# Moving one accumulating transfer, and the order of VectorE's list, in a fused convolution, GELU and projection kernel with Strassen blocks

## The chip, the core and the metric

The kernel runs on one core of one Trainium2 chip. The metric is device time in microseconds. Before the change it is 677.74 us, the median of 3 runs (676.55 to 678.93). Engines are named as in the profile: PE is TensorE, PEld its weight loads, DVE is VectorE, ACT is ScalarE, POOL is GpSimd, and SP is SyncE, which only issues transfers.

## The reference, cut to what matters

The input x holds 8 sequences of 4096 tokens with 192 channels. Each of 8 heads owns 24 channels and has 7 taps, normalised by a softmax. Every channel is convolved causally along its sequence with its head's taps. The result is a matrix of 32768 tokens by 192 channels. It goes through two dense layers with an exact GELU between them:

```python
w = np.exp(weight - weight.max(-1, keepdims=True))
w = w / (w.sum(-1, keepdims=True) + 1e-9)
conv = np.einsum('hk,bskhg->bshg', w, x_unfolded).reshape(B * S, D)
h = conv @ w_in                                   # 192 -> 2048
g = 0.5 * h * (1.0 + erf(h / sqrt(2)))
out = g @ w_out                                   # 2048 -> 192
```

## The kernel before, in words

**Tiling.** The tokens are split into two halves of 16384, which are worked on together. A half has 35 blocks: blocks 0 to 5 have 256 tokens per half, and blocks 6 to 34 have 512. For each block, SyncE loads x, VectorE transposes it to channels by tokens (function `trans`, letter t, L753), VectorE and in part ScalarE compute the seven taps (function `conv`, letter c, L781; ScalarE's share is L871), and TensorE multiplies by w_in (L998, into the PSUM tile hp). ScalarE applies GELU into the tile gT (L903), and TensorE multiplies by w_out into four PSUM banks of the tile ob.

**Stages.** TensorE works in a fixed order. While the first product of block n runs, in sixteen slices, the second product of block n − 1 is threaded between the slices. The document calls this stretch stage n. A slice holds 12 matmuls of the first product and a share of the second. In the even stages from 8 on the second product is the plain one of an odd block (`mm2_t`, L1076).

**Strassen blocks.** The even blocks 8, 10, ... 32 (list `ST`, thirteen of them) use a Strassen form of the second product, `mm2_s` (L1136), which runs in the odd stage behind them. It needs fewer matmuls, and in exchange sums of operands and of results. The operand sums are S1, S3, Dn and S4. S1 and S3 have four parts each, Dn and S4 two halves each. Dn is made from S1, and S4 from Dn. Parts 0 and 1 of S1 and parts 0, 1 and 2 of S3 are made by pairs of transfers that GpSimd issues: a copy of the first operand (L496), and behind its landing an accumulating transfer of the second operand (L499), both in `st_dma`. VectorE makes the other parts in `st_add` (L489): S1[2], S1[3], S3[3], Dn[0], Dn[1], S4[0], S4[1]. The list `DMAS` holds the places of the transfers in GpSimd's order, as (place, sum, part, first or second operand).

**Results of a Strassen block.** The products leave PSUM over the tiles p5s, uu, tq and gsm. ScalarE copies (`st_copy`, L528) at the slices in `AT_COPY`. VectorE makes four sums (`st_post`, letter p: P0 is L537, P1 is L541, P2 is L544, P3 is L548). GpSimd issues three transfers per block (`st_move`): p5s from its upper half to its lower one (L506), which P1 waits for; uu into gsm (L508), which P3 waits for; and the accumulating transfer of uu into tq (L511), called the tq transfer here. It waits until ScalarE's last copy (`S_AC`) and P0 to P2 (`S_DP`) are done. Three transposes on VectorE (L563, `st_evac`) bring the results to the tile osb: one from a bank and one from gsm (letter e, named E), and one from tq (letter q, the tq transpose), which waits for the tq transfer. SyncE's stores of the block wait for the tq transpose (`S_ET`), and so does ScalarE's first copy for the next Strassen block. The results of an odd block are transposed straight from three banks (`evac_t`, letter e, L377, named T0, T1, T2). T1 and T2 wait for the end of the whole second product (`S_MM2`), and each frees a bank for the Strassen product that follows.

**What sets the order.** VectorE executes the string `ORDER` letter by letter. Each letter takes the next piece of its lane: t, c, e, p and q as above, w for weight sums at the start, and 1, 3, d and 4 for VectorE's parts of S1, S3, Dn and S4. A piece that waits holds up all that follow. GpSimd's queue is sorted by pairs (block, place). The pairs of `DMAS` belong to block m; p5s stands at (m + 1, 8.5), gsm at (m + 2, 2), and the tq transfer at (m + 2, 14.1), behind all transfers for block m + 2. The copy of halo columns (`halo`, L674) for block n stands at (n − 2, 0). SyncE's queue in an odd stage begins at slice 4 and holds, in this order, four loads, the four stores of a Strassen block, four loads, and the four stores of an odd block.

A piece is named with its block in the following: c10.3b is tap 3 of block 10, second of two instructions; t12 is the transposing of block 12; E8 is a result transpose of block 8.

Of the kernel before, what the change touches and what calls it, by code (L numbers as in the profile page):

```python
# [11 lines left out]
def bass_lightweight_conv__then__act_gelu_exact_kernel(  # L12
# [59 lines left out]
    ST = list(range(M0 + 2, M1, 2))  # L72
# [46 lines left out]
    def ap(t, off, pat):  # L119
        return bass.AP(t, off, pat)  # L120

    with es:
# [139 lines left out]
        def part(q):  # L262

            return FQ * (0, 4, 2)[q], [[NP * F, 64], *([[F, NP]] if q < 2 else [[4 * FQ, 2 * NP]]), [1, FQ]]


        def cast(e, n, p):
            e.wait_ge(S_TR, NP * n + p + 1)
            dst = ap(xTb[PC[n]], p * XB + HX, [[NP * XB, 128], [1, WS[n]]])
            src = ap(xT[n % 2], p * XW + HX, [[NP * XW, 128], [1, WS[n]]])  # L270
            if n == 0:
                ins = e.activation(out=dst, in_=src, func=AF.Copy)
            else:
                ins = e.tensor_copy(dst, src)
            ins.then_inc(S_CAST[PC[n]])

        def dup(e, q, hf):

            c0, pat = part(q)
            e.wait_ge(S_WIN[(hf, 2 + 3 * hf, 3 + hf)[q]], 16)  # L280
            e.tensor_copy(
                ap(win, 64 * (1 - hf) * NP * F + c0 + FQ, pat), ap(win, 64 * hf * NP * F + c0, pat)
            ).then_inc(S_DUPP if (q, hf) == (0, 1) else S_DUPE)

        def trd(n):

            return NP * (n + 1) if n < 2 else 2 * NP + n - 1

        def cvd(n):

            return sum(NCV - 2 * (m in K0) for m in range(n + 1) if m not in PC)
# [273 lines left out]
        def load(e, n, qs=(0, 2, 1, 3), sm=None):  # L565
            mb = WS[n] // 32
            if n >= NX:
                e.wait_ge(S_TR, trd(n - NX))
            for q in qs:
                off = ((q // 2) * HALF + OFF[n]) * D + DQ * (q % 2)  # L570
                dst = [[TB // 32 * DQ, 32], [DQ, mb], [1, DQ]]
                src = [[D, 32], [32 * D, mb], [1, DQ]]
                e.dma_start(
                    ap(xin[n % NX], 32 * q * (TB // 32 * DQ), dst), ap(xt, off, src)
                ).then_inc(sm or S_XIN[n % NX], 16)

        def store(e, m):
# [29 lines left out]

        TAPS = ((5, 8, 11), (10, 12, 15))
        ORDER = (
            "tccccccccccccctccctccccccccccccwtccccccccccccwwwwwctcccccccccccctcccccccccccccccccccccccccettceccccc"  # L610
            "cccccccccetccccecccccccetcecc1ccde13de44ccccccpctpcpeccccccccpcccectec1cccd1e3de4q4ccccpcccptpcecccc"
            "ccccpcccectec1cccd1e3de4q4ccccpcccptpceccccccccpcccectec1cccd1e3de4q4ccccpcccptpceccccccccpcccectec1"
            "cccd1e3de4q4ccccpcccptpceccccccccpcccectec1cccd1e3de4q4ccccpcccptpceccccccccpcccectec1cccd1e3de4q4cc"
            "ccpcccptpceccccccccpcccectec1cccd1e3de4q4ccccpcccptpceccccccccpcccectec1cccd1e3de4q4ccccpcccptpceccc"
            "cccccpcccectec1cccd1e3de4q4ccccpcccptpceccccccccpcccectec1cccd1e3de4q4ccccpcccptpceccccccccpcccectec"
            "1cccd1e3de4q4ccccpcccptpceccccccccpcccececc1ccde13de44qccccpcccppepeqeeeeeee"
        )
        AT_COPY = {0: (1, 6), 1: (1, 8), 2: (1, 13), 3: (2, 1)}

        @block.gpsimd  # L620
        def _(g):
            def win_in(q, hf, sm):
                c0, pat = part(q)
                g.dma_start(
                    ap(win, 64 * hf * NP * F + c0, pat), ap(wint, c0 + FQ * hf, pat)
                ).then_inc(sm, 16)

            g.wait_ge(S_MSET, 1)
            for hf in range(2):
                m = idb[64 * hf : 64 * hf + 64, :]  # L630
                g.affine_select(
                    out=m,
                    in_=m,
                    compare_op=ALU.is_equal,
                    fill=0.0,
                    base=0,
                    pattern=[[-1, 64]],
                    channel_multiplier=1,
                ).then_inc(S_IDN)
            g.wait_ge(S_IDN, 2)  # L640
            g.memset(wnm[:, :], 0.0).then_inc(S_WNM)
            g.memset(ap(xTb[0], HF, [[NP * XB, 128], [XB, NP], [1, HB]]), 0.0).then_inc(S_HALO)
            for q in range(2):
                for hf in range(2):
                    win_in(q, hf, S_WIN[(hf, 2 + 3 * hf)[q]])
            g.wait_ge(S_PRO, 9)
            g.tensor_tensor(
                ap(dg, 3 * 64, [[KS * 64, 128], [64, KS - 3], [1, 64]]),
                ap(idb, 0, [[64, 128], [0, KS - 3], [1, 64]]),
                ap(wcol, 3, [[32, 128], [1, KS - 3], [0, 64]]),  # L650
                ALU.mult,
            ).then_inc(S_DG)

            def wout_in(k):
                g0, gs = ((0, 1), (4, 1), (2, 4), (3, 4))[k]
                g.dma_start(
                    ap(wout, 2 * g0 * C, [[NF * C, 128], [2 * gs * C, 2], [1, 2 * C]]),
                    ap(woutt, 256 * g0 * C, [[2 * C, 128], [256 * gs * C, 2], [1, 2 * C]]),
                ).then_inc(S_WOUT[k], 16)

            def halo(n):

                t, tw = (xTb[PC[n]], XB) if n in PC else (xT[n % 2], XW)
                dst = ap(t, HF, [[NP * tw, 128], [tw, NP], [1, HB]])
                if n >= 4:
                    g.wait_ge(S_CV, cvd(n - 2))
                if OFF[n] % SEQ == 0:
                    g.memset(dst, 0.0).then_inc(S_HALO)
                    return
                g.wait_ge(S_TR, trd(n - 1))  # L670
                src = ap(
                    xT[(n - 1) % 2], HF + WS[n - 1], [[NP * XW, 128], [XW, NP], [1, HB]]
                )
                g.tensor_copy(dst, src).then_inc(S_HALO)  # L674

            win_in(2, 0, S_WIN[3])
            load(g, 2, (0,), S_XP)
            halo(1)
            g.wait_ge(S_HALO, 2)
            dup(g, 0, 1)  # L680
            win_in(2, 1, S_WIN[4])
            wout_in(0)
            load(g, 2, (2,), S_XP)
            g.wait_ge(S_DUPP, 1)
            cast(g, 1, 0)
            cast(g, 1, 1)
            load(g, 2, (1,), S_XP)
            wout_in(1)
            cast(g, 1, 2)
            load(g, 2, (3,), S_XP)  # L690
            wout_in(2)
            wout_in(3)
            halo(2)
            work = [((n - 2, 0), halo, n) for n in range(3, NB)]
            for m in ST:
                for at, name, q, h in DMAS:
                    work.append(((m, at), st_dma, g, m, name, q, h))
                work += [((m + 1, 8.5), st_move, g, m, 0), ((m + 2, 2), st_move, g, m, 1)]
                work.append(((m + 2, 3 if m == ST[-1] else 14.1), st_move, g, m, 2))
            for _, op, *rest in sorted(work, key=lambda q: q[0]):  # L700
                op(*rest)

# [549 lines left out]
```

## Time and profile before

| Quantity | Value |
|---|---|
| Median of 3 runs | 677.74 us |
| The profiled execution, its own time | 676.95 us |
| Its span, first to last instruction | 675.2 us |
| PE busy | 666.1 us |
| DVE busy | 611.7 us |
| ACT busy | 595.6 us |
| POOL busy | 196.0 us |
| Granted clock of TensorE | 1.00 of full speed in every stretch asked for |

The page gives busy time, its share of the span and the number of instructions per engine. The view of waits has lines of the form "engine, tile and line that waited <- what it waited for: us in total, times, longest us". A timeline row gives the start and the length in us, the engine, the line, the operation, the tiles, the shape, the number of instructions, and in brackets the idle time in front and what ended it. What ended a wait is inferred, and for a wait on several things only one is named. A row of the view by windows gives the stretch, its length, the busy time of PE, PEld, DVE, ACT and POOL with numbers of instructions, then the granted clock, the busy share of the transfer engines and GB/s. A row of the issues of transfers ends with the median time from issue to landing.

### The profile page before, as it was taken

Reading aid. Unit: us, or ns where it says so; the run is one execution under the profiler, and the core shown is the slowest. Engines: PE = TensorE matmul, PEld = TensorE weight load, DVE = VectorE, ACT = ScalarE, POOL = GpSimd, SP = SyncE. Lnnn points to the kernel's source line nnn. Section 1 sums busy time; section 2 is a strip of 40 time slices with the busy share of each in tenths; the row PEclk is TensorE's granted clock in tenths of the full one; section 3 lists DMA queues with packets and bytes.
Section 4 is the critical chain, followed back from the end, with each engine's and each line's share of the span. In section 5 each row is a group of like instructions: output and inputs, shape, how many; then the busy total and the mean of one; then the engine's idle time right before and its main releaser. Section 6 shows DMA issues by size and latency. Waiting matters only on the chain.

```text
span 675.2 us, 27463 instructions
## 1 busy us (share of the span) xinstructions
PE 666.1 (99%) x12504; PEld 462.8 (69%) x12504; DVE 611.7 (91%) x704; ACT 595.6 (88%) x681; POOL 196.0 (29%) x230
## 2 busy tenths in 40 slices
PE   9999999999998999999999999999999999999998
PEld 8899655565675767666666676766666667676767
DVE  5999998889898999998999999999989999999721
ACT  8899988898997989989898898988989889898883
POOL 7000702314133151332605225051340613315000
PEclk9999999999999999999999999999999999999999
DMA  9435352676947659486785856769476694836433
GB/s 150 111 96 132 72 107 66 136 160 143 217 110 131 151 142 213 115 169 144 142 193 131 173 127 148 172 150 180 124 150 156 150 193 113 159 104 143 114 73 94
DMA packets 159076, 93.72 MB, mean 139 GB/s; under 512 B 129089, under 2 KB 152449, under 8 KB 158961
## 3 DMA queue, kind: packets, MB, share of 16 engines
q1 hardware_dynamic: 129136, 49.37, 33.4%
q0 software_dynamic: 28704, 42.02, 28.9%
q8 instruction: 98, 1.61, 1.0%
q10 hardware_dynamic: 1120, 0.59, 0.3%
q14 instruction: 18, 0.14, 0.1%
HBM read 28.31 MB, written 25.17 MB: 79 GB/s over the span
## 4 chain that ended last, share of the span: by engine, by line
PE 71%; DVE 9%; issue 8%; DMA 7%; POOL 4%; ACT 1%; SPq 0%; DVEq 0%; POOLq 0%; ACTq 0%
PE hp L998 36%; PE ob L1076 17%; PE ob L1136 13%; DVE acc L781 4%; PE ob L1038 4%; DVE sst L489 2%; DMA sst<-gT 2%; POOL sst L499 2%; DMA tq<-uu 2%; DMA xin<-in_x_dram 2%; DMA p5s<-p5s 1%; DVE xT L753 1%; PE ob L1192 1%; PE hp L1192 1%; DVE xc L781 1%
## 5 line engine op out<-in xcount | busy, mean ns | idle before, releaser
L903 ACT ACTIVATE gT<-hp 128x1024 bf16<-128x1024 f32 x510 | 514.5, 1022 | 63.2 <-PE hp L998 57.2
L998 PE MATMUL hp<-xc,win 64*64 64x512 bf16 (+2 forms) x6036 | 441.9, 366 | 1.1 <-DVE xc L781 1.0
L781 DVE SCALAR_TENSOR_TENSOR acc<-xT,wcol,acc 128x1024 f32<-128x1024 f32 (+1 forms) x330 | 298.2, 962 | 5.3 <-ACT acc L871 4.5
L998 PEld LDWEIGHTS hp<-xc,win 64*64 64x64 bf16 (+1 forms) x6036 | 217.7, 106 | 105.5 <-ACT gT L903 8.2
L1076 PE MATMUL ob<-gT,wout 64*64 64x512 bf16 x2880 | 201.1, 376 | 0.0
L1136 PE MATMUL ob<-gT,wout 64*64 64x512 bf16 x1248 | 164.5, 376 | 0.0
L1076 PEld LDWEIGHTS ob<-gT,wout 64*64 64x64 bf16 x2880 | 106.8, 118 | 51.3
L1136 PE MATMUL ob<-sst,wst 64*64 64x512 bf16 x624 | 131.0, 376 | 0.0
L499 POOL DMA_DIRECT2D sst<-gT x65 | 82.2, 1265 | 71.5 <-DMA sst<-gT 70.8
L1136 PEld LDWEIGHTS ob<-gT,wout 64*64 64x64 bf16 x1248 | 79.8, 118 | 24.0
L753 DVE STREAM_TRANSPOSE xT<-xin 128x1536 f32<-128x1536 f32 (+2 forms) x39 | 74.7, 1926 | 3.3 <-DMA xin<-in_x_dram 3.2
L674 POOL COPY xT<-xT 128x18 f32<-128x18 f32 x30 | 37.7, 1256 | 106.6 <-DVE xc L781 100.2
L496 POOL DMA_DIRECT2D sst<-gT x65 | 50.9, 783 | 52.2 <-ACT gT L903 51.9
L489 DVE TENSOR_TENSOR sst<-gT,sst 128x2048 bf16<-128x2048 bf16 x52 | 62.6, 1207 | 0.0
L781 DVE SCALAR_TENSOR_TENSOR xc<-xT,wcol,acc 128x1024 bf16<-128x1024 f32 (+1 forms) x66 | 61.1, 966 | 0.0
L871 ACT ACTIVATE acc<-xT,wcol 128x512 f32<-128x512 f32 (+1 forms) x87 | 61.1, 702 | 0.0
L1136 PE MATMUL ob<-gT,wst 64*64 64x512 bf16 x208 | 57.4, 376 | 0.0
L1136 PEld LDWEIGHTS ob<-sst,wst 64*64 64x64 bf16 x624 | 53.7, 107 | 5.0
L377 DVE STREAM_TRANSPOSE osb<-ob 128x512 f32<-128x512 f32 x45 | 39.7, 884 | 13.1 <-PE ob L1076 12.9
L1136 PE MATMUL ob<-sst,wout 64*64 64x256 bf16 x416 | 46.4, 270 | 4.4 <-DVE sst L489 4.4
L1136 PEld LDWEIGHTS ob<-sst,wout 64*64 64x64 bf16 x416 | 34.8, 119 | 12.3 <-DVE sst L489 8.6
L506 POOL DMA_DIRECT2D p5s<-p5s x13 | 7.5, 575 | 118.0 <-ACT p5s L528 108.7
(74 smaller groups left out, 331.4 us busy)
## 6 DMA issues: line engine op xcount, KB each, us to landing
sst<-gT POOLq DMA_DIRECT2D x130, 256.0 KB, 3.6
out_dram<-osb SPq DMA_DIRECT2D x124, 192.0 KB, 3.8
xin<-in_x_dram SPq DMA_DIRECT2D x116, 192.0 KB, 4.2
tq<-uu POOLq DMA_DIRECT2D x13, 256.0 KB, 4.5
xin<-in_x_dram SPq DMA_DIRECT2D x18, 96.0 KB, 2.5
gsm<-uu POOLq DMA_DIRECT2D x13, 128.0 KB, 2.3
p5s<-p5s POOLq DMA_DIRECT2D x13, 64.0 KB, 4.7
wout<-in_moe_w_out_dram POOLq DMA_DIRECT2D x4, 192.0 KB, 4.9
```

The source lines that it names most:

```text
L377: v.transpose(osb_t(m, j), bank(BK[m][j])).then_inc(S_EV)
L489: v.tensor_tensor(out, one, two, ALU.add).then_inc(S_SA[NS.index(name)])
L496: e.dma_start(out, one).then_inc(S_CP[name, q], 16)
L499: e.dma_start(out, two, accum_op=ALU.add).then_inc(S_AD[name, q], 16)
L674: g.tensor_copy(dst, src).then_inc(S_HALO)
L753: v.transpose(out, src).then_inc(S_TR)
L781: ins = v.scalar_tensor_tensor(dst, src, wk, a, op0=ALU.mult, op1=ALU.add)
L871: a.activation(out=acc[n % 2][:, p * TB : p * TB + w], in_=ap(xT[n % 2], p * XW + HX, [[NP * XW, 128], [1, w]]), func=AF.Copy, scale=wcol[ ...
L903: a.activation(out=ap(gT[n % 2], i * c * 2 * w, dst), in_=ap(ob, 2 * TB, [[4 * TB, 128], *src[1:]]) if u < SL0[1] and u % 3 == 2 else ap(h ...
L998: ins = t.matmul(hbuf(u, slice(fo, fo + fw), o, w), ap(win, f1, [[NP * F, 64], [2, fw]]), xc[n % 2][r, p * TB : p * TB + w], start=(p == 0 ...
L1076: ins = t.matmul(bank(BK[m][j], slice(64 * h, 64 * h + 64), w), ap(wout, 64 * hf * NF * C + CH[h][i] * C + j, [[NF * C, 64], [NP, 64]],), ...
L1136: ins = t.matmul(bank(BK[m][bk], slice(64 * cg, 64 * cg + 64), w), wt_, a[r, c0 : c0 + w], start=(e == mine[0]), stop=(e in (mine[-1], GRO ...
```

## The change

Two things change. In GpSimd's queue the tq transfer for block m moves from (m + 2, 14.1) to (m + 2, 8.2): from behind the last transfer of the sums for block m + 2 to just behind the accumulating transfer of S1 part 0, which stands at 8.1. For the last Strassen block it stays at (34, 3). In VectorE's list, in the odd stages 11 to 33, the tq transpose of the block before and T1 move ahead of S1[3], and S1[3] moves ahead of Dn[0]. One steady stage, cut out of the two strings:

```
before: c.2a c.2b c.3a  Dn0  S1[3]  T1  S3[3]  Dn1  T2  S4[0]  tq transpose  S4[1]  c.3b
after:  c.2a c.2b c.3a  tq transpose  T1  S1[3]  Dn0  S3[3]  Dn1  T2  S4[0]  S4[1]  c.3b
```

In stage 33 the tq transpose stood behind S4[1]; it is moved to the same place as in the others. Around the first Strassen block three more pieces move: c10.3b goes from behind S4[1] to ahead of Dn[0], T1 of block 7 goes behind S1[3], and P1 of block 8 goes ahead of t12, as it is in the other blocks. At the start the weight copy w1 moves from behind block 4's taps to behind the first of them.

```diff
@@ ORDER @@
-            "tccccccccccccctccctccccccccccccwtccccccccccccwwwwwctcccccccccccctcccccccccccccccccccccccccettceccccc"
-            "cccccccccetccccecccccccetcecc1ccde13de44ccccccpctpcpeccccccccpcccectec1cccd1e3de4q4ccccpcccptpcecccc"
...
+            "tccccccccccccctccctccccccccccccwtcwcccccccccccwwwwctcccccccccccctcccccccccccccccccccccccccettceccccc"
+            "cccccccccetccccecccccccetcecc1cccd1e3de44cccccpcptcpeccccccccpcccectec1cccqe1d3de44ccccpcccptpcecccc"
...
@@ block.gpsimd @@
                 work += [((m + 1, 8.5), st_move, g, m, 0), ((m + 2, 2), st_move, g, m, 1)]
-                work.append(((m + 2, 3 if m == ST[-1] else 14.1), st_move, g, m, 2))
+                work.append(((m + 2, 3 if m == ST[-1] else 8.2), st_move, g, m, 2))
```

## The prediction

> **What bounds the kernel now.** I read the page first, then the waits between 126 and 641 us (the stretch in which Strassen results are made), then the timelines of TensorE, VectorE and GpSimd around the longest of those waits. The page says that TensorE is nearly always busy and VectorE close behind:
>
> ```profile
> PE 666.1 (99%) x12504; PEld 462.8 (69%) x12504; DVE 611.7 (91%) x704; ACT 595.6 (88%) x681; POOL 196.0 (29%) x230
> ```
>
> The waits name what is left to win. TensorE waits for operand sums (L489), and VectorE waits for two transfers, p5s and tq:
>
> ```profile
> PEld ob L1136 <- DVE sst L489: 8.6, 10, 2.9
> ...
> DVE tq L541 <- DMA p5s<-p5s: 6.4, 7, 1.7
> DVE osb L563 <- DMA tq<-uu: 5.4, 4, 2.2
> PE ob L1136 <- DVE sst L489: 4.4, 5, 2.5
> ```
>
> Call stage n the stretch from the first L998 matmul of block n to that of block n+1; times "in the stage" count from its start. Stages without a Strassen product take 20.72 to 20.80 us. The Strassen stages 9, 11, ... 33 take 19.87 at best (9, 17, 33); the others exceed that by 0.28 (11), 2.76 (13), 0.06 (15), 0.71 (19), 0.36 (21), 0.30 (23), 0.57 (25), 1.32 (27), 0.56 (29), 0.30 (31): together 7.22 us. That is the most that this change can win in the steady part. Three of these stages by their windows (length first, then busy PE):
>
> ```profile
> 207.87:230.50 22.63, 20.17 (x388) 13.85 (x384) 19.44 (x22) 18.63 (x22) 3.68 (x5) 1.00 0.91 174
> 292.02:311.88 19.86, 19.86 (x388) 13.94 (x384) 18.10 (x21) 18.56 (x22) 2.71 (x5) 1.00 0.93 192
> 497.20:518.39 21.19, 20.18 (x388) 13.68 (x384) 18.12 (x21) 18.64 (x22) 4.23 (x5) 1.00 0.84 179
> ```
>
> All the excess sits at one place, the seventh of the sixteen slices, where the first matmul wants the second half of S4. Stage 13 on VectorE, then on TensorE:
>
> ```profile
> 213.74 1.20 DVE L489 TENSOR_TENSOR sst<-gT,sst 128x2048 bf16<-128x2048 bf16 x1
> 217.16 0.85 DVE L563 STREAM_TRANSPOSE osb<-tq 128x512 f32<-128x512 f32 x1 [2.22 <-DMA tq<-uu]
> 217.90 1.17 DVE L489 TENSOR_TENSOR sst<-gT,sst 128x2048 bf16<-128x2048 bf16 x1
> ```
> ```profile
> 219.12 0.31 PE L1136 MATMUL ob<-sst,wout 64*64 64x256 bf16 x1 [2.46 <-DVE sst L489]
> ```
>
> VectorE stands 2.22 us before the tq transpose, the S4 sum behind it ends 11.20 us into the stage, and TensorE starts 0.05 us later. Over all stalled stages the end of that sum less the excess is 8.43 or 8.44 us. So excess = end of the second S4 sum − 8.43, or nothing if it ends sooner. What sets that end is a fully busy VectorE list that begins at the tq sum of L541, which waits for the p5s transfer in the Strassen stage before:
>
> ```profile
> 349.89 0.42 DVE L541 TENSOR_TENSOR tq<-ob,p5s 64x256 f32<-64x256 f32 x1 [1.07 <-PE ob L1136]
> 350.23 2.32 DVE L753 STREAM_TRANSPOSE xT<-xin 128x1536 f32<-128x1536 f32 x1
> ```
>
> (p5s landed at 349.79, 0.10 us before; the view names TensorE, whose part was long done.) The sum starts R us before its stage ends, and where no tq wait follows, the next Strassen stage's excess is 3.67 − R: R = 2.95 gave 0.71, 3.30 gave 0.36, 3.37 gave 0.30, 3.10 gave 0.56. I use that line below.
>
> **The change part by part.** *The tq transfer on GpSimd.* It is one DMA issue, moved from behind the last S3 transfer to behind S1 part 0's second transfer. In stage 20:
>
> ```profile
> 365.65 1.20 POOL L499 DMA_DIRECT2D sst<-gT  x1 [0.21 <-issue]
> 367.68 1.22 POOL L499 DMA_DIRECT2D sst<-gT  x1 [0.82 <-DMA sst<-gT]
> ...
> 373.85 1.18 POOL L499 DMA_DIRECT2D sst<-gT  x1 [3.01 <-DMA sst<-gT]
> 374.56 1.38 POOL L511 DMA_DIRECT2D tq<-uu  x1
> ```
>
> It now starts at about 366.36 (issues without a wait follow 0.71 apart), 8.2 us sooner. Its own waits, the negated copy and the third tq sum, are over three microseconds into the stage, so it blocks nothing. Its landing takes 3.3 to 6.3 us, so it is in by 372.7 at the latest, and the tq transpose will ask at about 374.8: that wait goes everywhere. Behind it on the queue stand four sum transfers (S1 part 1, S3 parts 2, 1, 2) and the halo copy. Their lag is between nothing and 1.4 us: two accumulating transfers without a pause land 2.1 us (369.25, 371.35) or 1.2 us (373.56, 374.77) apart, 0.7 of the first pair was a wait. I take 1.4. A part is wanted in the slice of the next stage in which its first matmul stands (slices last 1.30, 1.30, 1.08 us in turn, TensorE's L998 half first). S1 part 1 lands at 18.0 to 19.7 in stages of 20.8 and is wanted at 21.6; S3 part 1 by 24.0, wanted at 25.4; S3 part 2 at 23 to 25.5, wanted at 27.5. Cost 0; only before stage 13 (26.77) could 0.7 us show, ahead of a stall there and so not on top of it. The halo copy gets earlier.
>
> *VectorE's list in a Strassen stage.* The set of instructions up to the second S4 sum is the same in steady stages: before Dn0, S1[3], T1, S3[3], Dn1, T2, S4[0], tq transpose, S4[1]; after tq transpose, T1, S1[3], Dn0, S3[3], Dn1, T2, S4[0], S4[1]. Without waits S4[1] ends when it did. Inside, S1[3] ends about 0.4 us later (2.2 us behind the slot's start instead of 1.8), wanted 3.15 into the stage; it would have ended at 2.2 to 3.4 there, so a few tenths of the stall move forward and none is added. S3[3], T2 and S4[0] come 0.8 later, each still ahead of its need. In stage 33 the transpose now precedes S4[1]: 6.79 + 0.78 = 7.57, under 8.43. In stage 9 c10.3b does: 6.78 + 0.65, also under.
>
> So without tq waits (0.55, 2.22, 0.86, 1.73 us in stages 11, 13, 25, 27) the S4[1] sum ends at 8.17, 8.98, 8.14 and 8.02. Excess then: 0, 0.55, 0, 0. Gain 0.28 + 2.21 + 0.57 + 1.32 = 4.38 us. ScalarE's wait for the tq transpose (2.7 us in two stages, 13 and 27) lies inside these.
>
> *The swap for the first Strassen block.* Before, the 2.57 us transpose t12 ran while p5s was in flight, and the list later stood 1.37 us for TensorE at the E8 transpose. After, the p5s sum comes first, so VectorE idles from 140.2 to 142.9. Then the third tq sum ends near 147.2 instead of 145.05, and the second product of block 9 wants it at 146.7: 0.5 us. The remainder is in the line above (R = 3.23 gives 0.44 in stage 11), which counts from that same delayed TensorE. Ends 0 and 0.75; I take 0.55.
>
> *Moved weight copy w1.* 0.41 us earlier in the list delays block 4's sums by that; TensorE's only waits for xc before Strassen are at 27.26, and VectorE stands 1.70 us at 117.53. Cost 0.
>
> *Store and load traffic.* SyncE's stores of a Strassen block wait for the tq transpose. They go out at 7.8 to 8.8 us in the stage (10.2 in stage 13); after, at 6.9 as in stage 9, which has no such wait. The second set of loads then starts at about 10.0 instead of 10.3 to 11.2, when p5s is issued at 11.5. This cost no row of before shows in a steady stage; p5s landings lasted 3.5 us where no loads run (33) to 5.4 (17). I bound it by leaving R as in the rows (the ten stages 13 to 31 then have 2.85 us in all, a mean of 0.28) and by stage 9 for all (R = 3.23, 0.44 each, 4.4). Nearest in traffic is stage 9, nearest in everything else the rows: I take 0.36 each, so 0.8 us lost.
>
> Sum: 4.38 − 0.55 − 0.8 = 3.0 us. The profiled execution took 676.95 us (675.2 of them span), 0.8 under the median 677.74; on the median, 674.8.
>
> **The rivals.** *p5s lands as in the rows or sooner.* Its transfer is small and gets past the loads; for it speak stages 15, 23, 25 (3.6 to 4.4 us) although loads were out. Then 4.38 − 0.55 = 3.8 gain, 673.9, and with all landings at 3.6 nothing is left but the swap: 6.7 gain, 671.1. [...]
>
> *The gain is spent on p5s.* Stores and loads that run ahead are queued on the same engines, and the completion of p5s comes behind more of them. At 5.2 to 5.4 us in every stage R is about 3.1 to 2.95, excess 0.57 to 0.72, ten times 0.6 plus 0.55: 6.6, gain 0.6, time 677.1. [...]
>
> *Slower, by that mechanism alone.* Place: L541 in each Strassen stage. Break-even is an excess of 0.67 in all ten (R = 3.0, landing 5.3 us); beyond 5.5 us the time passes +0.3%. At 5.7 us: 0.9 each, 9.0 + 0.55 against 7.22, +2.3 us, 680.1. Against it: no landing was over 5.4.
>
> *The tq transpose still waits.* The transfer would have to take over 8 us; the longest took 6.3. I give it no chance of its own.
>
> **How the numbers follow.** A measurement tells about 0.3% (2.0 us) from no change. Forecast (674.8, with 673.5 to 675.7 around it) 0.50; p5s sooner (about 672.5) 0.13; gain spent (about 677) 0.26; slower (680) 0.11. The range reaches from the middle of the second case to the third's upper part, 672.3 to 677.7. Faster 0.63, same 0.26, slower 0.11.
>
> **What would show it.** VectorE's wait for tq<-uu gone from the list of waits; ScalarE's wait at L528 too; stages 13 and 27 near 20.3; the rest of TensorE's waits for L489 in the seventh slice. Wrong if p5s lands more than 5.3 us after issue throughout, if S1 or S3 transfers become what TensorE waits for, or if T1 waits for TensorE at the head of the stage.

## The result, and the profile after

The changed kernel takes 674.44 us, the median of 17 runs (672.25 to 677.71), against 678.38 us for the kernel before in as many (672.92 to 686.61). The ratio is 0.994, with a 95% interval from 0.9918 to 0.9963: faster by 0.6%, with the whole interval below 1. The forecast was 674.8. The profiled executions differ by less, 674.2 against 676.95 us (spans 672.5 and 675.2); the second profile of the kernel before, further down, bears on this.

The engines of the changed kernel, from its page, and then the waits between 126 and 641 us:

```profile
PE 666.5 (99%) x12504; PEld 473.6 (70%) x12504; DVE 611.5 (91%) x704; ACT 595.6 (89%) x681; POOL 197.1 (29%) x230
```
```profile
DVE tq L541 <- DMA p5s<-p5s: 11.3, 8, 2.9
...
PEld ob L1136 <- DVE sst L489: 5.5, 11, 0.7
...
PE ob L1136 <- DVE sst L489: 1.0, 4, 0.3
```

No line for tq<-uu is left, where there were 5.4 us, nor one for ScalarE's wait on the tq transpose. The longest wait of TensorE for an operand sum fell from 2.5 to 0.3 us in the PE line. What grew is VectorE's wait for p5s. By windows, stages 10, 13, 17 and 27 (length, then busy time of PE, PEld, DVE, ACT, POOL, then clock, transfer share, GB/s):

```profile
145.63:166.97 21.34, 20.90 (x388) 14.54 (x384) 21.25 (x24) 18.74 (x22) 10.72 (x12) 1.00 0.57 131
207.69:227.81 20.12, 20.12 (x388) 13.91 (x384) 18.84 (x22) 18.53 (x22) 4.47 (x4) 1.00 0.88 180
289.91:310.95 21.04, 20.57 (x388) 13.83 (x384) 20.07 (x23) 18.53 (x22) 2.08 (x4) 1.00 0.79 169
496.06:516.03 19.97, 19.97 (x388) 13.88 (x384) 18.66 (x21) 18.52 (x22) 3.21 (x4) 1.00 0.88 180
```

The reader is to compare the lengths with those before: stages 13 and 27 are 2.51 and 1.22 us shorter, stage 17 is 1.18 longer, and stage 10 is 0.6 longer. The excess of the odd stages over 19.87 us fell from 7.2 to 4.2 us; that of the even ones over 20.72 rose from 0.7 to 1.6; stage 7 began 0.6 sooner. Together −2.8 us, the whole difference of the two spans. The last of these is not shown to come from the change: in the nine profiled kernels that share the changed start of the list, stage 7 begins anywhere from 83.9 to 85.8 us.

The tq transfer in stage 20 is issued where it was expected, 13.0 us into the stage instead of 21.4:

```profile
364.06 1.24 POOL L499 DMA_DIRECT2D sst<-gT  x1
364.80 1.44 POOL L511 DMA_DIRECT2D tq<-uu  x1
```

It landed 17.4 us into the stage. The four sum transfers behind it landed 0.6 to 1.3 us later than before in this stage, and the list of waits has no line in which TensorE waits for one.

### The profile page after: what moved, and what is told of

It is laid out like the page before. It is cut to its first block, busy times and chain, and to the rows that moved or that the text cites. A ratio compares the mean times of both kernels' runs of the same rounds, so it can differ in the third digit from the quotient of the medians.

```text
span 672.5 us, 27463 instructions
## 1 busy us (share of the span) xinstructions
PE 666.5 (99%) x12504; PEld 473.6 (70%) x12504; DVE 611.5 (91%) x704; ACT 595.6 (89%) x681; POOL 197.1 (29%) x230
## 4 chain that ended last, share of the span: by engine, by line
PE 28%; DVE 14%; issue 10%; DMA 3%; POOL 3%; ACT 1%; DVEq 0%; POOLq 0%
PE hp L998 14%; PE ob L1076 7%; PE ob L1136 6%; DVE acc L781 6%; DVE sst L489 3%; DMA p5s<-p5s 2%; POOL sst L499 2%; DVE xT L753 1%; DMA sst<-gT 1%; DVE osb L377 1%; DVE xc L781 1%; PE ob L1192 1%; PE hp L1192 1%; DVE osb L563 1%; ACT gT L903 0%
## 5 line engine op out<-in xcount | busy, mean ns | idle before, releaser
L998 PEld LDWEIGHTS hp<-xc,win 64*64 64x64 bf16 (+1 forms) x6036 | 224.5, 106 | 98.6 <-ACT gT L903 7.4
L1076 PEld LDWEIGHTS ob<-gT,wout 64*64 64x64 bf16 x2880 | 109.0, 118 | 49.9 <-issue 1.4
L499 POOL DMA_DIRECT2D sst<-gT x65 | 84.7, 1303 | 71.4 <-DMA sst<-gT 71.0
L1136 PEld LDWEIGHTS ob<-gT,wout 64*64 64x64 bf16 x1248 | 82.2, 118 | 21.0
L496 POOL DMA_DIRECT2D sst<-gT x65 | 52.9, 813 | 50.6 <-ACT gT L903 50.6
L674 POOL COPY xT<-xT 128x18 f32<-128x18 f32 x30 | 35.1, 1170 | 105.8 <-DVE xc L781 100.1
L489 DVE TENSOR_TENSOR sst<-gT,sst 128x2048 bf16<-128x2048 bf16 x52 | 62.1, 1217 | 0.0
L506 POOL DMA_DIRECT2D p5s<-p5s x13 | 7.4, 572 | 116.2 <-ACT p5s L528 107.6
L1038 PE MATMUL ob<-wout,gT 64*128 64x192 bf16 x768 | 41.3, 243 | 0.0
```

The lines of the kernel that those rows point to most:

```text
L489: v.tensor_tensor(out, one, two, ALU.add).then_inc(S_SA[NS.index(name)])
L496: e.dma_start(out, one).then_inc(S_CP[name, q], 16)
L499: e.dma_start(out, two, accum_op=ALU.add).then_inc(S_AD[name, q], 16)
L998: ins = t.matmul(hbuf(u, slice(fo, fo + fw), o, w), ap(win, f1, [[NP * F, 64], [2, fw]]), xc[n % 2][r, p * TB : p * TB + w], start=(p == 0 ...
L1038: ins = t.matmul(bb[sub], gT[m % 2][r, c0 : c0 + 128], wout[r, CH[sub][i] * C : (CH[sub][i] + 1) * C], start=(ph == 0 and k == 0), stop=(p ...
L1076: ins = t.matmul(bank(BK[m][j], slice(64 * h, 64 * h + 64), w), ap(wout, 64 * hf * NF * C + CH[h][i] * C + j, [[NF * C, 64], [NP, 64]],), ...
```

## The experiments

Two theories were at odds about the gain (the vanished tq wait, or VectorE's order), and two about what is left (the start of VectorE's list after p5s, or something else). "Excess" and R are those of the prediction: the time of a stage over 19.87 us, and the time before the end of a Strassen stage at which the tq sum of L541 starts.

**The transfer alone.** VectorE's list is that of before.

```diff
 (kernel before)
-  ... 3 if m == ST[-1] else 14.1), st_move, g, m, 2))
+  ... 3 if m == ST[-1] else 8.2), st_move, g, m, 2))
```

> Only the tq transfer is moved; VectorE's list is that of before. My theory: the gain is the wait of the tq transpose that goes away, and the order inside a steady stage is neutral up to the second S4 sum. Then no wait for tq<-uu is left, the excess over 19.87 us in the odd stages is about 4 us in all as in the changed kernel, and stages 10 and 11 lose the 0.5 us of the first-block swap: about 673.9 us. Rival: the gain comes from VectorE's list, its own sums ahead of the work on transferred ones. Then this kernel stays at 677 to 678 us.

It took 672.66 us (671.36 to 675.28), ratio 0.9893 to before (0.985 to 0.9936). There is no wait for tq<-uu, and the excess in the odd stages is 4.7 us in all. Stages 10 and 11 have none. The whole gain belongs to the transfer; the list adds nothing that shows. With the list the median is 1.8 to 2.1 us higher (674.44, and 674.75 in the repeat below). The first-block swap is 0.6 to 0.8 us of that; the ranges overlap, and the rest is not shown to be a cost of the list.

**The list alone.** The transfer stays at 14.1.

```diff
 (changed kernel)
-  ... 3 if m == ST[-1] else 8.2), st_move, g, m, 2))
+  ... 3 if m == ST[-1] else 14.1), st_move, g, m, 2))
```

> Only VectorE's list is changed; the tq transfer stays behind the sum transfers. My theory: the tq transpose now stands at 0.6 us in the odd stage, the transfer lands 4.4 to 9.3 us into it, so VectorE waits 4 us or more in each of the stages 11 to 33, the second S4 sum ends at 12 to 13 us instead of 8.5, and TensorE stalls some 4 us in eleven stages: about 720 us. Rival: the list pays by itself: 674 to 678 us.

It took 752.2 us (two runs; ratio 1.1057, 1.0971 to 1.1142). The direction was right, the size too small, and the place another. VectorE waits 44.9 us for tq<-uu, and the twelve stages 11 to 33 have 79.3 us of excess instead of some 45. (In the kernel before the transfer landed 3.4 to 9.3 us into these stages, where the expectation has 4.4 to 9.3.) In stage 21 VectorE stands at the tq transpose, and TensorE waits in the third slice for S1[3], which the new list puts behind that transpose, and not in the seventh for S4:

```profile
407.21 0.85 DVE L563 STREAM_TRANSPOSE osb<-tq 128x512 f32<-128x512 f32 x1 [4.08 <-DMA tq<-uu]
```
```profile
409.33 0.40 PE L1136 MATMUL ob<-sst,wst 64*64 64x512 bf16 x1 [4.04 <-DVE sst L489]
```

In all twelve stages the fourth slice begins late, by 55.4 us together or 4.6 in each. Most of the remainder is TensorE's clock. In stage 21 the windows show what follows the idle stretch (the clock is the number behind the five engines):

```profile
404.60:409.20 4.60, 0.69 (x13) 0.14 (x3) 1.99 (x4) 1.30 (x2) 0.00 (x0) 1.00 0.52 90
409.20:411.00 1.80, 1.67 (x28) 1.11 (x32) 1.80 (x4) 0.34 (x1) 0.00 (x0) 0.87 0.00 0
411.00:413.50 2.50, 2.50 (x30) 1.31 (x24) 2.50 (x4) 1.00 (x2) 0.00 (x0) 0.50 0.43 108
```

Here half the clock is granted 1.2 us after the idle stretch, when TensorE is busy again; in eight of the eleven stages that have it, it begins while TensorE still idles. Half of the time at half the clock, counted from the fourth slice on, is 22.3 us. That leaves 1.6 of the 79.3 us, and in each of the eleven stages with half the clock the two parts give the excess within 0.1 us. (The mean clock of the run, 0.959 over 748.7 us, gives 30.7 us; that counts half the clock during idle time as well.)

**The first-block swap undone.** In the changed kernel, P1 of block 8 goes back behind t12.

```diff
 ORDER, around block 8
-  P0  c10.6b  P1  t12  c11.1a  P2  E8
+  P0  c10.6b  t12  P1  c11.1a  P2  E8
```

> The changed kernel with P1 of block 8 back behind t12. My theory: the third tq sum of block 8 is done in time, stage 10 goes from 21.34 back to 20.7 to 20.8 us, and stage 11 stays at 19.9 to 20.1: stages 10 and 11 together 40.7 us instead of 41.27; the total is about 0.5 us lower, which the time alone cannot tell. Rival: the 0.55 us of stage 10 comes from the tq transfer's new place (the first one is issued in stage 10), then stage 10 stays at 21.3.

Stage 10 went from 21.34 to 20.72 us and stage 11 was 19.87: 40.6 us together. The median, 674.12 us (ratio 0.9911, 0.9875 to 0.9946), cannot tell 0.6 us: the runs lie 4.2 us apart, and in the profiled one the odd stages have 6.0 us of excess instead of 4.2. VectorE in the changed kernel, and then here:

```profile
142.53 0.42 DVE L541 TENSOR_TENSOR tq<-ob,p5s 64x256 f32<-64x256 f32 x1 [2.92 <-DMA p5s<-p5s]
142.88 2.29 DVE L753 STREAM_TRANSPOSE xT<-xin 128x1536 f32<-128x1536 f32 x1
145.09 1.24 DVE L781 SCALAR_TENSOR_TENSOR acc<-xT,wcol,acc 128x1024 f32<-128x1024 f32 x1
146.36 0.43 DVE L544 TENSOR_TENSOR tq<-ob,p5s 64x256 f32<-64x256 f32 x1
```
```profile
139.31 2.32 DVE L753 STREAM_TRANSPOSE xT<-xin 128x1536 f32<-128x1536 f32 x1
142.23 0.42 DVE L541 TENSOR_TENSOR tq<-ob,p5s 64x256 f32<-64x256 f32 x1 [0.61 <-DMA p5s<-p5s]
142.57 1.27 DVE L781 SCALAR_TENSOR_TENSOR acc<-xT,wcol,acc 128x1024 f32<-128x1024 f32 x1
143.87 0.42 DVE L544 TENSOR_TENSOR tq<-ob,p5s 64x256 f32<-64x256 f32 x1
```

With the transpose behind it, the wait for p5s is 2.92 us instead of 0.61, and the third tq sum (L544) starts 0.7 us into stage 10 instead of 1.3 us before it.

**One tap behind the sums.** In the steady odd stages of the changed kernel c.3a goes behind the second S4 sum.

```diff
 ORDER, each steady odd stage
-  c.2a c.2b c.3a  Q T1 S1[3] Dn0 S3[3] Dn1 T2 S4[0] S4[1]  c.3b
+  c.2a c.2b  Q T1 S1[3] Dn0 S3[3] Dn1 T2 S4[0] S4[1]  c.3a c.3b
```

> The changed kernel with one tap instruction (c.3a, 1.2 us) moved from ahead of the tq transpose to behind the second S4 sum in the eleven steady odd stages. My theory: TensorE's excess is the end of that sum less 8.43 us; the sum now ends 1.2 us sooner, at 7.3 to 8.4, so the excess of 4.2 us in the odd stages goes to nothing (at most 0.5 us in all): about 670.3 us. Rival 1: the sum is not what is left, TensorE would wait for S1 or S3 parts or T1 waits for TensorE at the head of the stage and eats the 1.2 us: 673 to 674.5 us. Rival 2: VectorE as a whole is the bound, so work that is put off comes back as a late xc for the next first product: 674 us or more.

(Q is the tq transpose.) It took 670.58 us (669.01 to 671.88), ratio 0.9855 (0.9809 to 0.9901). The excess in the odd stages is 1.4 us, down from 4.2. That is not the nothing that was expected, and TensorE's wait has a new name:

```profile
PEld ob L1136 <- DVE tq L537: 2.5, 6, 0.7
```

In the five stages with excess left (13, 17, 21, 25, 29) the first tq sum P0 (L537) ends at 13.19 us plus the excess. So the next constraint is P0, which TensorE wants 4.76 us later in the stage than the second S4 sum.

**The p5s copy one slice sooner**, in the changed kernel.

```diff
-        AT_COPY = {0: (1, 6), 1: (1, 8), 2: (1, 13), 3: (2, 1)}
+        AT_COPY = {0: (1, 6), 1: (1, 7), 2: (1, 13), 3: (2, 1)}
```

> The changed kernel with ScalarE's copy into p5s before slice 7 instead of slice 8, so the p5s transfer is issued at about 10.4 us in the odd stage instead of 11.5 to 12.7. My theory: the landing of p5s starts VectorE's full list and so sets what is left of the excess; VectorE idles 0.3 to 2.1 us there, about 1.1 on the mean, so the list starts about 1 us sooner, R grows to 4 or more, and the excess of 4.2 us falls under 1 us: about 671 us. Rival: p5s lands when SyncE's loads let it, near the third load at 16 to 17 us, whenever it is issued; then R stays at 3.2 and the time at 674 us.

It took 671.97 us (671.35 to 673.42), ratio 0.9884 (0.9846 to 0.9922). R rose to 4.5 to 5.3 us, and no wait of TensorE for L489 is left. The 3.6 us of excess that remain are another thing: 0.27 or 0.28 in every one of the thirteen odd stages, even 9 and 33, where TensorE now waits for ScalarE:

```profile
PEld hp L998 <- ACT gT L903: 15.7, 49, 0.6
```

(7.1 us in 32 times in the changed kernel.) In stage 9 the copy, at its new place, stands ahead of the GELU whose end TensorE then waits for.

**SyncE's second traffic later**, in the changed kernel.

```diff
-                    sp.wait_ge(S_MM1, SL0[at[0]] + 4)
+                    sp.wait_ge(S_MM1, SL0[at[0]] + (4 if at[1] < 1 else 12))
```

> The changed kernel, with SyncE's second four loads and second four stores of an odd stage held back to slice 12 (about 14 us in the stage; they went at 10.3 to 16.5). My theory: p5s lands late because of the load traffic queued ahead of it; with less of it, landing falls from 4.9 us to 3.5 us or less, as in stage 33 that has no loads, R grows by over 1 us, and the excess goes under 0.5 us: about 670.5 us if the later stores and loads hold nothing else up. Rival: landing stays over 4.5 us, so the traffic is not its cause, and the time stays at 674 us.

It holds back the second four loads and the four stores of an odd block, which now begin 14.7 us into the stage. Two runs took 669.18 and 668.82 us, ratio 0.9847 (0.9772 to 0.9923). The last line of the view of L506 in the changed kernel, and here:

```profile
DMA to landing us min/median/max: 2.5/4.8/6.0
```
```profile
DMA to landing us min/median/max: 1.9/3.4/4.1
```

R rose to 4.2 to 5.1 us, and the excess of all odd stages fell to 0.1 us. So this traffic on SyncE's queue does lengthen the landing of p5s, and the landing sets what was left. Which of the two, loads or stores, does it was not separated.

**One tap, the swap and P0.** To the kernel with one tap behind the sums, two edits are added.

```diff
 ORDER, each steady odd stage, behind S4[1]
-  c.3a c.3b c.4a c.4b c.5a  P0  c.5b c.6a c.6b  P1
+  c.3a c.3b c.4a c.4b  P0  c.5a c.5b c.6a c.6b  P1
 and the first-block swap undone, as above
```

> The kernel with one tap instruction behind the second S4 sum, with two more edits: the first-block swap undone, and the first tq sum (P0) one tap sooner (ahead of c.5a). My theory: what was left there, 1.4 us in the odd stages, came from P0 ending later than 13.19 us in the stage, which holds up P4's first matmul; P0 now ends at about 12.1. No excess is left in the odd stages, stage 10 is at 20.72: about 668.8 us. Rival: P0 waits for ScalarE's p5s copy or VectorE's list stalls elsewhere, and the excess stays over 1 us: 670.5 us.

It took 669.18 us (668.11 to 670.15), ratio 0.9849 (0.9807 to 0.9891). Neither odd nor even stages have any excess; the list of waits between 126 and 641 us has no line any more in which TensorE waits for VectorE or a transfer. p5s still takes 4.8 us to land: here the slack is on VectorE's side.

**The changed kernel once more**, measured beside the three kernels above.

> The changed kernel once more, beside the others on one chip. About 674.4 us; ratio to before 0.990 to 0.996; stage 10 at about 21.3 again, and about 4 to 5 us excess in the odd stages.

674.75 us (673.43 to 676.16), ratio 0.9938 (0.9909 to 0.9966); excess 4.5 us in the odd stages and 1.5 in the even ones, stage 10 at 21.56. The kernel with SyncE's traffic later and the one with all three list edits are 5.6 to 5.8 us below this, which is about the 6.0 us of excess that they lack.

**The kernel before once more**, for a second profile.

> The kernel before once more, for a second profile. The medians of many runs moved by 3.9 us, the two profiled executions only by 2.75. My theory: the tq wait varies from execution to execution, and the profiled execution of before (676.95 us) was one with little of it; in this one the tq transposes wait as long as the time is over 673 us or so, and the excess in the odd stages grows with it: 676 to 685 us, tq waits of 4 to 12 us in all. Rival: the waits are the same 5.4 us and the difference lies elsewhere (the start, or stages without a Strassen product).

The profiled execution took 684.38 us. VectorE's waits for tq, and TensorE's for the sums:

```profile
PEld ob L1136 <- DVE sst L489: 12.8, 9, 3.4
DVE osb L563 <- DMA tq<-uu: 10.1, 4, 3.7
```

The excess in the odd stages is 14.8 us, of which stages 11 and 13 have 4.75 and 4.82. In stage 11 the second S4 sum ended at 11.51 us, which explains 3.08; the other 1.67 follow the idle stretch of TensorE, at half the clock:

```profile
176.00:179.30 3.30, 0.95 (x21) 0.69 (x25) 2.91 (x4) 1.50 (x2) 0.00 (x0) 1.00 1.02 183
179.30:182.80 3.50, 3.50 (x41) 1.82 (x37) 2.73 (x4) 2.49 (x3) 0.57 (x1) 0.51 0.94 233
```

So the wait that the change removes varies from execution to execution, and the one that the prediction was made from had little of it: it lay 1.4 us below the median of its kernel, the profiled one of the changed kernel only 0.2 below. That is the difference between 3.9 us by the medians and 2.75 by the profiled executions. The runs without a profile agree: in 33 of the 59 executions of the kernel before that have their clock on record, its mean is 0.995 to 0.998, which in this profile (0.995) means two such stretches at half the clock; in all 29 of the changed kernel it is 1.00. Why the tq transfer is late in some executions is not shown. Counted from the start of stage 12 it was issued at 23.9 us in both profiles and landed 6.7 us later here, 6.2 in the first one; from the start of stage 10 it was issued at 23.9 and 22.7 us and landed 6.5 and 4.8 us later.

**Both cures together**: the one tap, the swap, P0, and SyncE's second traffic later.

> The kernel with the shifted tap, the first-block swap undone and P0 one tap sooner, and SyncE's second traffic at slice 12 as well. My theory: each of the two removed all excess by itself, so nothing is left for the other: 668.5 to 669.5 us, the same as either alone. Rival: they add up, since stages without excess could still get shorter: under 667 us.

668.78 us (667.96 to 670.63), ratio 0.982 (0.9763 to 0.9878). They don't add: no stage from 8 to 33 has any excess left, so these waits have nothing more to give.

## Why the prediction was right, point by point

*The sum.* The mechanism was right, and the closeness of the time is in part luck. By the stages of the two profiled executions, the change is worth 4.1 us for the tq wait, −0.6 for the swap, −1.1 in the other odd stages and −0.2 in even stages: 2.2 us, where the sum had 3.0. The other 0.6 of the measured 2.75 is the earlier start of stage 7, which is not shown to be an effect of the change. By the medians the gain is 3.9 us, more than forecast, since the tq wait was priced from an execution that had little of it.

*The tq wait goes: 4.38 us.* Right. In its four stages (11, 13, 25, 27) the excess fell by 0.22, 2.51, 0.15 and 1.22, together 4.1 us. In stage 25 only 0.15 of the expected 0.57 came, since p5s landed later in stage 23 (4.96 us after issue instead of 4.25). Moving the transfer alone removed the wait too.

*The line from the second S4 sum.* Right. The end of that sum less the excess is 8.43 or 8.44 us in every stalled stage of the changed kernel, of the transfer alone and of the kernel with the swap undone. The earlier form, 3.67 − R, holds within 0.1 us in most stages and misses where the even stage between was itself longer. In stage 11 it gives 0.57, measured 0.06, behind the 0.6 of stage 10. In stage 17 it gives 1.44, measured 1.18, behind 0.24 more in stage 16: p5s took 6.0 us in stage 15, the third tq sum came late, and the next second product waited. The prediction named this wait for block 8 alone.

*The four transfers behind tq, cost 0; lag up to 1.4 us.* Right: 0.6 to 1.3 in stage 20, and no wait. (Of the two pairs behind the 1.4 us, the one 1.2 us apart, 373.56 and 374.77, is a copy and the accumulating transfer behind it.) *S1[3] later moves a stall forward and adds none.* Right in stage 17, where 0.42 us of the 1.18 stand in the third slice and the sum of both is what the S4 line gives.

*The first-block swap, 0.55 us.* Right: stage 10 grew by 0.62, and undoing the swap removed it.

*The weight copy w1, cost 0.* Nothing contradicts it: stage 7 takes 20.75 us in both profiles, and the start before it varies by more than any cost of this size.

*Store and load traffic, 0.8 us.* The size was near, the step was not. In the seven other stages that had no tq wait and no stall from it (15 to 23, 29, 31) the excess rose from 2.3 to 3.4 us, by 1.1 (for the ten stages 13 to 31 the forecast was 3.6 in all, and they have 4.1). The mean p5s landing in stages 11 to 31 rose from 4.56 to 4.88 us. But SyncE's stores didn't go at 6.9 us: they went at 7.4 to 8.0 in most stages, since the fourth load ahead of them was mostly issued at 6.2 to 7.4 us (5.95 in stage 9), and the second loads of stages 15 to 25 and 29 began at 10.6 us on the mean, against 10.7 before. That this traffic lengthens the landing is shown by holding it back. That it was the change's earlier stores which raised it by 0.3 us isn't: the other kernels with an early tq transfer have 4.8 to 5.0 us, the two profiles of before 4.6 and 4.4, and the cause of this difference stays open.

*The rivals.* The sooner p5s didn't come, and the spent gain did so only in part: it needed a landing of 5.2 to 5.4 us in every stage, and the mean was 4.88. The limit of 5.3 us was passed in one stage only, at 6.0. That p5s gets past loads that are out, as the first rival has it, the traces hardly show: in the kernel before it landed ahead of a load issued sooner in stages 15 and 25 alone, by 0.03 and 0.44 us, and in the changed one in stages 25, 27 and 29, by 0.03 to 0.17. In the other odd stages it landed behind all that SyncE had issued ahead of it, as the second rival has it. With the second traffic held to 14.7 us the landing fell from 4.8 to 3.4 us, but p5s, issued at 11.45 us in most stages, was in at 14.1 to 15.5, before this traffic began or just after: the traffic was absent and not merely shallower. The order of landing agrees with the shorter landing time, without being shown to be the cause. In the slower rival one sum is off by the prediction's own line: a landing of 5.7 us makes R = 2.6 and the excess 1.07 in each stage instead of 0.9, so about +4.0 us instead of +2.3.

## What to carry to other kernels

When an engine executes a fixed list, find the last wait before the starved consumer, and write the stall as one line (end of the producer less a constant). It told here how much the tq wait was worth, what remained (p5s), and, with its own constant, which constraint came next (P0). A transfer that is ready early should not stand in a queue behind others that wait (moved alone, it gave a ratio of 0.9893 here); and a list that is reordered to use an early landing is very expensive without the move that makes it early (752.2 us here). Before a cost is priced from one profile, it is worth a second one: the wait removed here was 5.4 us in one execution and 10.1 in another.

## What the runs showed of the hardware that was not expected

In these runs a longer stall of TensorE cost more than its length: in stage 11 of the second profile of before the late S4 sum explains 3.08 us of 4.75. An idle stretch of 2.46 us (stage 13 of the first profile of before), by the modelled ends of matmuls, left the clock at 1.00. All stretches of 2.75 us and more (2.75 and 2.96 in the second profile of before, 3.02 to 5.96 in the kernel with the list alone) brought half the clock (0.50 and 0.51 in the windows above), for 3.4 us (0.51 over 3.50 us in the window of the second profile) or 6.8 us in the records of granted clock. It began inside the stretch, at the earliest 2.25 us after its start, or up to 1.2 us behind its end. Where TensorE was busy throughout, 3.4 us at half the clock cost 1.7 us (stages 11 and 21 of the list alone); of the 6.8 us a part fell into the idle time, and the cost was 1.3 to 2.6. What sets these lengths is not shown.
